# Reordering value products, transposes and a third gate-score broadcast in a windowed-attention and mixture-of-depths kernel

## The chip, the core and the metric

The kernel runs on one core of a Trainium2 chip. A core has five engines with separate instruction streams: TensorE (PE; its weight loads are shown as PEld), VectorE (DVE), ScalarE (ACT), GpSimd (POOL) and SyncE (SP, here only a DMA queue). TensorE writes to PSUM, a memory of 8 banks, from which VectorE or ScalarE fetch the results. The metric is the device time of one execution in microseconds. The profile is of a separate execution and is somewhat longer.

## What is computed

Two stages follow each other. The first is attention with a sliding window of 128 keys and 4 always visible "sink" keys, over 4 batches, 8 heads, 768 positions and 64 values per head:

```python
keep = (pos[None, :] < n_sink) | ((rel >= 0) & (rel < window))   # rel = query - key
scores = np.where(keep, scale * q @ k.T, -1e9)
a = softmax(scores)
x = a @ v                              # then heads side by side: [4, 768, 512]
```

The second stage picks, in each batch, the 128 positions with the highest gate score and adds a gated feed-forward result to those alone:

```python
scores = np.einsum('bsd,d->bs', x, w_gate)
top_idx = np.argpartition(-scores[b], 128)[:128]
ye = np.maximum(x[b, top_idx] @ w1, 0.0) @ w2          # 512 -> 1024 -> 512
out[b, top_idx] = x[b, top_idx] + sigmoid(scores[b, top_idx])[:, None] * ye
```

## The kernel before

The order of the work is written out by hand (`tc.manual_schedule`): each engine executes its instructions in the order in which the program calls them, and waits are set where data or buffers demand it.

**Steps.** The main loop (L619) has 30 steps. A step deals with one block j of 128 queries of one batch. Batch 0 is done in two passes over half of the heads (steps 0 to 5 and 6 to 11), batches 1 to 3 in one pass each (steps 12 to 17, 18 to 23, 24 to 29). In a step come, in this order on TensorE: the scores for the step two later (`step_scores`), the value products of the step (`values`), and then what is registered for the step in `todo` by `at(i, f)`, in the order of registration. Work is also hung in with `before` (ahead of the scores), `middle` (between scores and values) and `late` (at the step's end). VectorE normalises the values (`norm`, L290) straight after the value products, and the next step's value products need the same PSUM bank pair X, so they wait for this norm.

**Value products.** `values` (L253) multiplies in float32, which gives two matmul records for each call. First come the sinks (L272, tiles of 64x64), then products of full blocks (128 rows, 64 columns), and last the half blocks (64x64), which cover the edges of the window; half-block products also read the value chunk of block j+1.

**Transposes.** Keys and queries of two heads are cast to bf16 by `cast_pair` (L134), transposed on TensorE by `transposes` (L166) through banks Y and Y+1 and copied to `KT` and `QT` by VectorE (L177) or ScalarE (L179). The first scores of a batch, two steps ahead of its first block, need all of its pairs; the last pair is transposed at steps 9, 15 and 21. Ahead of the loop, pairs 0 and 2 of batch 0 are transposed with `fill` matmuls on zeros between, which keep TensorE busy.

**Ranking.** A position is chosen if fewer than 128 gate scores of its batch are higher. There are two ways to compare all 768 scores with all. For batches 0 and 1 the scores go out to a row in DRAM (`bounce_out`, L305) and come back broadcast over all partitions into `sbc` (`bounce_in`, L308), both through GpSimd's DMA queue; six `rank_c` (L311) on VectorE then count. For batches 2 and 3, `spread` (L315) broadcasts 128 scores by a TensorE matmul and a ScalarE copy to `sbl`, `compare` counts on VectorE, and `overtake` and `overtaken` add what later blocks contribute. `select` builds a one-hot matrix from the ranks, `choose` turns it into row numbers and starts the gather of the rows, and `ffn` hangs the feed-forward stages into three following steps. GpSimd's queue also loads the feed-forward weights (`load_weights`, before step 22), gathers and scatters.

Of the kernel before, what the change touches and what calls it, by code (L numbers as in the profile page):

```python
# [9 lines left out]
BF16 = mybir.dt.bfloat16  # L10
# [7 lines left out]
S = 768  # L18
D = 64
HP = H // 2  # L20
NB = S // 128
# [7 lines left out]
LO, HI, FULL = slice(0, 64), slice(64, 128), slice(0, 128)  # L29
# [4 lines left out]
def kernel(  # L34
# [14 lines left out]
    pe, dve, act, pool, sp = nc.tensor, nc.vector, nc.scalar, nc.gpsimd, nc.sync  # L49
# [6 lines left out]
    def one(shape, dt, name):  # L56
        return cp.tile(shape, dt, name=name, tag=name)
# [3 lines left out]
    X, Y = 4, 6  # L61
# [4 lines left out]
    raw = [one([128, 2, NB, D], FP32, f"raw{i}") for i in range(8)]  # L66
# [7 lines left out]
    xb = x0[:, 0:NB // 2, :].bitcast(BF16).rearrange("p a (t n) -> p (a t) n", t=2)  # L74
    E2 = x0[:, NB - 1, :].bitcast(BF16)[:, 0:NB * 128].rearrange("p (c n) -> p c n", n=128)
    sbc = one([128, S], FP32, "sbc")
    sbl = one([128, S], FP32, "sbl")
    G = one([128, 21 * 128], BF16, "G")
    junk = one([128, DM], FP32, "junk")
    less = one([128, NB], FP32, "less")  # L80
    rankl = [one([128, NB], FP32, "rankl"), x0[:, NB - 2, 40:40 + NB]]
    ones_b = one([128, 1], BF16, "ones_b")
    rank = one([128, NB], FP32, "rank")
    E = one([128, NB, 128], BF16, "E")
# [23 lines left out]
    srow = tc.dram_tile([B, S], FP32, name="srow")  # L108
# [12 lines left out]
    st = [State(b) for b in range(B)]  # L121
# [41 lines left out]
            sp.dma_start(out=vb[r, h0:h0 + 2, c, 0:D],  # L163
                         in_=v[0, 4 + h0:6 + h0, k0:k0 + 64, :].rearrange("h p d -> p h d"))

    def transposes(b, hp, bank):  # L166
        s = st[b]
        n = slot[(b, hp)]
        for t, (src, dst) in enumerate(((kq[2 * n], s.KT), (kq[2 * n + 1], s.QT))):
            trp = ps[:, bank + t, :].bitcast(BF16).rearrange("p (c n) -> p c n", c=8)  # L170
            for c in range(NB):
                pe.transpose(out=trp[:, c, :], in_=src[:, c, :, :].rearrange("p h d -> p (h d)"),  # L172
                             identity=ident_b[:, :])
            o = dst[:, hp, :].rearrange("d (p c) -> d p c", c=NB)
            i = trp[:, 0:NB, :].rearrange("d c p -> d p c")
            if t == 0 and (b == 0 or hp % 2 == 0):
                dve.tensor_copy(out=o, in_=i)  # L177
            else:
                act.copy(out=o, in_=i)  # L179

    def sink_keys(b, hp):
        s = st[b]
# [70 lines left out]
    def values(b, j, heads, bank, which):  # L253
        s = st[b]
        p = {i: ptn.get((b, i)) for i in (j - 1, j, j + 1)}
        seen = set()
        a, z = heads[0], heads[-1] + 1

        def mm(be, c, hh, rows, i, slot, kc):
            h = 4 * be + hh  # L260
            key = (be, c)
            pe.matmul(out=ps[64 * c:64 * c + 64, bank + be, hh * SK:hh * SK + SK],  # L262
                      lhsT=p[i][rows, h, 64 * slot:64 * slot + 64], rhs=s.v[be][rows, hh, kc, 0:SK],
                      start=key not in seen, stop=False, skip_group_check=True)
            seen.add(key)

        for be in range(2):
            for c in range(2):
                if j < 2 - c:
                    continue  # L270
                r = (LO, HI)[be ^ c]
                pe.matmul(out=ps[64 * c:64 * c + 64, bank + be, a * SK:z * SK],  # L272
                          lhsT=s.psk[which][r, c, 64 * (j - 1):64 * j], rhs=vsk[r, b, be, a:z, :],
                          start=True, stop=False, skip_group_check=True)
                seen.add((be, c))
        for hh in heads:
            if j:
                mm(0, 0, hh, FULL, j - 1, 2, j - 1)
            mm(0, 1, hh, FULL, j, 1, j)
        for hh in heads:  # L280
            mm(1, 0, hh, FULL, j, 1, j)
            mm(1, 1, hh, FULL, j, 2, j)
        for hh in heads:
            mm(0, 0, hh, LO, j, 0, j)
            mm(1, 1, hh, LO, *((j + 1, 0) if j < NB - 1 else (j, 3)), j + 1)
            if j:
                mm(0, 1, hh, HI, j - 1, 3, j - 1)
                mm(1, 0, hh, HI, j - 1, 3, j - 1)

    def norm(x, heads, bank):  # L290
        a, z = heads[0], heads[-1] + 1
# [14 lines left out]
        pool.dma_start(out=srow[b, :].rearrange("(p c) -> p c", c=NB), in_=st[b].scol[:, :])  # L306

    def bounce_in(b):  # L308
        pool.dma_start(out=sbc[:, :], in_=srow[b, :].partition_broadcast(128))

    def rank_c(b, c):  # L311
        dve.tensor_scalar(out=junk[:, :].bitcast(BF16)[:, 0:S], in0=sbc[:, :], scalar1=st[b].scol[:, c:c + 1],  # L312
                          scalar2=0.0, op0=ALU.is_gt, op1=ALU.add, accum_out=rank[:, c:c + 1])

    def spread(b, j, bank):  # L315
# [27 lines left out]
    def select(e, rk, c0, c1):  # L343
        n = c1 - c0
        dve.tensor_tensor(out=e[:, c0:c1, :], in0=iota_f[:, :].unsqueeze(1).to_broadcast((128, n, 128)),
                          in1=rk[:, c0:c1].unsqueeze(2).to_broadcast((128, n, 128)), op=ALU.is_equal)
# [23 lines left out]
    def gate_end(b):  # L370
        g = gt[b]
        dve.tensor_scalar_add(out=g[:, :], in0=g[:, :], scalar1=1.0)
        dve.reciprocal(out=g[:, :], in_=g[:, :])
# [38 lines left out]
    def scatter(b):  # L412
        pool.indirect_dma_start(out=flat[0:(b + 1) * S, :],
                                out_offset=bass.IndirectOffsetOnAxis(ap=idx[b][:, 0:1], axis=0),
                                in_=ys[b][:, :], in_offset=None, bounds_check=(b + 1) * S - 1, oob_is_err=False)

    with tc.manual_schedule():
# [24 lines left out]
        def fill(n):  # L442
            for i in range(n):
                pe.matmul(out=ps[:, i % 4, :], lhsT=zb[:, 0:128], rhs=zb[:, :], start=True, stop=True,
                          skip_group_check=True)
# [17 lines left out]
        cast_pair(0, 2, dve, act)  # L463

        fill(10)
        transposes(0, 0, Y)
        fill(5)
        transposes(0, 2, X)
        fill(2)

        steps = [(0, j, g) for g in range(2) for j in range(NB)]
        steps += [(b, j, None) for b in range(1, B) for j in range(NB)]
        todo = {}
# [3 lines left out]

        def at(i, f):
            todo.setdefault(i, []).append(f)

        def late(i, f):
            todo_late.setdefault(i, []).append(f)

        def middle(i, f):
            mid.setdefault(i, []).append(f)
# [47 lines left out]
        def choose(b, bank, e=E):  # L533
            keep[b] = chosen(b, bank, e)
            gate(b, keep[b])
            gather(b)

        def ranks(b, last):

            for j in range(last):  # L540
                at(start(b) + j + 1, lambda j=j: spread(b, j, 2))
                late(start(b) + j + 1, lambda j=j: compare(b, j))

        def overtaking(b, js, bank):
            overtake(js, bank)
            overtaken(b, js[-1], bank)


        for b, i, js in ((0, 12, (15, 15, 16, 17, 17, 18)), (1, 18, (20, 21, 22, 23, 24, 25))):
            middle(i, lambda b=b: bounce_out(b))  # L550
            middle(i + 1, lambda b=b: bounce_in(b))
            for c, i_c in enumerate(js):
                late(i_c, lambda b=b, c=c: rank_c(b, c))
        late(19, lambda: select(E, rank, 0, NB))
        at(20, lambda: choose(0, 3))
        at(21, lambda: gate_end(0))
        ranks(2, NB)
        at(25, lambda: overtaking(2, range(1, NB), 3))
        late(25, lambda: select(E, rank, 0, NB))
        at(26, lambda: choose(1, 3))  # L560
        late(26, lambda: select(E2, rankl[0], 0, NB))
        at(27, lambda: gate_end(1))
        at(27, lambda: choose(2, 3, E2))
        at(28, lambda: gate_end(2))
        for b in range(B - 1):
            at((12, 18, 24)[b], lambda b=b: token_cols(b))
        before(22, load_weights)
# [6 lines left out]
        for b, at_ in ((1, (0, 1, 2, 3)), (2, (6, 8, 9, 11)), (3, (13, 14, 15, 16))):  # L574
            for hp, i in enumerate(at_):
                before(i, lambda b=b, hp=hp: load_pair(b, hp))
        at(2, lambda: transposes(0, 1, Y))
        at(3, lambda: transposes(0, 3, Y))
        at(3, lambda: sink_keys(0, 1))
        at(3, lambda: sink_keys(0, 3))  # L580
        at(4, lambda: sink_scores(0, (1, 3), 1, Y))
        for b, i0 in ((1, 6), (2, 12), (3, 18)):
            for hp in range(HP):
                before(i0 + hp - 2, lambda b=b, hp=hp: cast_pair(b, hp))
                at(i0 + hp, lambda b=b, hp=hp: transposes(b, hp, Y))
                at(i0 + hp, lambda b=b, hp=hp: sink_keys(b, hp))
            at(i0 + 4, lambda b=b: sink_scores(b, range(HP), 0, Y))

        def ffn(b, i):
            before(i, lambda: ffn_cast(b))  # L590
            at(i, lambda: ffn_in(b, Y))
            at(i + 1, lambda: ffn_1(b, 0, Y + 1))
            at(i + 1, lambda: ffn_1(b, 1, Y))
            for half in range(2):
                at(i + 2, lambda half=half: ffn_2(b, half, Y + 1))
            at(i + 2, lambda: ffn_out(b, Y + 1))
        ffn(0, 24)
        ffn(1, 27)
        late(28, lambda: scatter(0))
        late(29, lambda: scatter(1))  # L600
        before(29, lambda: ffn_cast(2))
        at(29, lambda: ffn_in(2, Y))
# [12 lines left out]
                        in_=own4[0:16, :].unsqueeze(1).to_broadcast((16, 2 * B, HP)))  # L615
        pool.tensor_copy(out=vsk[64:80, :, :, :, :].rearrange("p b e h d -> p (b e h d)"),
                         in_=vsk[0:16, :, :, :, :].rearrange("p b e h d -> p (b e h d)"))
# [39 lines left out]
        b = B - 1  # L657
# [64 lines left out]
```

## Time and profile before

| | |
|---|---|
| time, median of 3 | 144.41 us (143.46 to 145.68) |
| span of the profiled execution | 149.5 us |
| TensorE granted clock, mean | 0.958 |
| DMA traffic | 32.42 MB, 217 GB/s on average |

How the stretches differ, in 10 us windows (engine busy us, and mean busy share of the 16 DMA engines):

| us | PE | DVE | ACT | DMA share |
|---|---|---|---|---|
| 0 to 10 | 5.84 | 6.43 | 3.65 | 0.87 |
| 30 to 40 | 8.40 | 6.43 | 6.57 | 0.99 |
| 60 to 70 | 8.18 | 6.14 | 5.99 | 0.95 |
| 80 to 90 | 9.62 | 9.18 | 7.00 | 0.69 |
| 100 to 110 | 7.62 | 8.69 | 5.13 | 1.02 |
| 120 to 130 | 9.79 | 7.35 | 3.28 | 0.49 |
| 140 to 150 | 3.46 | 1.36 | 1.20 | 0.24 |

Busy time of TensorE is modelled from pipelined matmuls, so gaps between the starts of its records tell more than its busy share. In a line of the timeline the columns are start and length in us, engine, line of the program, operation, tiles written and read, shapes, and how many records were merged; a bracket at the end tells how long the engine had been idle and who ended that. In a list of waits the three numbers are total us, how often, and the longest. Batch 0 ends near 48 us, batch 1 near 74, batch 2 near 101, the last value products near 129; the rest is the feed-forward work on the chosen rows of the last two batches.

### The profile page before, as it was taken

The numbers are of one execution on the slowest core, as the hardware profiler recorded it, in microseconds if no ns is written. First come the engines' busy times: TensorE is split into PE (matmuls) and PEld (weight loads), VectorE is DVE, ScalarE is ACT, GpSimd is POOL, SyncE is SP. The second block draws the span as 40 slices with busy tenths as digits, with TensorE's granted clock in tenths as the row PEclk, the third lists the DMA queues.
The fourth block names the chain that finished last, engine by engine and source line by source line (L and its number), as shares of the span: only waits on it lengthen the run. The fifth ranks groups of instructions, "written<-read, shape, count | busy, mean of one in ns | idle before, by whom it ended". The sixth has DMA issues, their size and how long they took to land. (4 is left out here: it accounts for less than half of the span.)

```text
span 149.5 us, 6406 instructions
## 1 busy us (share of the span) xinstructions
PE 122.4 (82%) x2759; PEld 93.0 (62%) x2759; DVE 90.3 (60%) x283; ACT 79.0 (53%) x106; POOL 60.8 (41%) x103
## 2 busy tenths in 40 slices
PE   6479798988779794968998997989599999987930
PEld 2146676677657682756776786768498578665700
DVE  6822145364835841637699898689882797576420
ACT  3064936666588756546665966566526243232310
POOL 8805902955275271109514633800130426550510
PEclk9956999999999999999999999999968999999997
DMA  3999959999999999997985664899950426441221
GB/s 97 373 195 360 237 144 365 393 222 273 280 292 364 359 285 349 351 292 218 256 229 149 178 196 150 115 181 230 273 189 12 153 95 203 189 175 39 52 91 70
DMA packets 41147, 32.42 MB, mean 217 GB/s; under 512 B 26768, under 2 KB 35984, under 8 KB 41120
## 3 DMA queue, kind: packets, MB, share of 16 engines
q1 hardware_dynamic: 37984, 26.22, 58.6%
q0 software_dynamic: 2592, 5.02, 14.9%
q10 hardware_dynamic: 544, 0.79, 1.5%
q8 instruction: 21, 0.34, 0.9%
q14 instruction: 6, 0.05, 0.1%
HBM read 25.20 MB, written 8.92 MB: 228 GB/s over the span
## 5 line engine op out<-in xcount | busy, mean ns | idle before, releaser
L262 PE MATMUL ps<-vbuf,pt 64*64 64x65 f32 (+1 forms) x1440 | 47.4, 227 | 7.6 <-issue 6.9
L262 PEld LDWEIGHTS ps<-vbuf,pt 64*64 64x64 f32 (+1 forms) x1440 | 40.1, 135 | 19.5 <-issue 15.5
L251 ACT ACTIVATE pt<-ps 128x1024 f32<-128x1024 f32 x48 | 47.3, 1033 | 6.9 <-PE ps L229 5.6
L295 DVE RECIPROCAL rz<-ps 128x8 f32<-128x8 f32 (+1 forms) x30 | 5.9, 198 | 39.0 <-PE ps L262 39.0
L186 POOL COPY ksk<-KT 64x4 bf16<-64x4 bf16 x32 | 9.3, 292 | 38.2 <-DVE KT L177 27.5
L141 POOL CAST kq<-raw 128x768 bf16<-128x768 f32 x28 | 22.6, 849 | 2.0 <-DMA raw<-in_k_dram 1.5
L213 PE MATMUL ps<-QT,KT 64*64 64x192 bf16 (+2 forms) x384 | 17.8, 249 | 5.1 <-ACT QT L179 2.4
L298 DVE TENSOR_TENSOR x<-ps,rz 128x256 f32<-128x256 f32 (+1 forms) x60 | 19.5, 366 | 1.2
L179 ACT COPY QT<-ps 128x768 bf16<-128x768 bf16 x16 | 12.8, 803 | 11.6 <-PE ps L172 11.6
L302 DVE CUSTOM_DVE_ANT_0 junk<-x,wgb 128x512 f32<-128x512 f32 x24 | 18.0, 751 | 0.4
L272 PE MATMUL ps<-vsk,psk 64*64 64x260 f32 (+1 forms) x180 | 15.6, 346 | 1.7 <-DVE x L298 1.4
L213 PEld LDWEIGHTS <-KT 64*64 64x64 bf16 x384 | 10.6, 108 | 10.3 <-issue 6.1
L172 PE MATMUL ps<-ident_b,kq 128*128 128x128 bf16 x192 | 14.6, 228 | 2.9 <-ACT kq L139 2.0
L229 PE MATMUL ps<-mask,ident_b 64*64 64x256 bf16 (+1 forms) x208 | 15.4, 263 | 0.0
L172 PEld LDWEIGHTS <-kq 128*128 128x128 bf16 x192 | 11.9, 102 | 4.9 <-ACT kq L139 2.2
L312 DVE TENSOR_SCALAR_CACHE_REDUCE junk<-sbc,scol 128x768 bf16<-128x768 f32 x12 | 12.2, 1013 | 0.4
L177 DVE COPY KT<-ps 128x768 bf16<-128x768 bf16 x10 | 9.5, 952 | 3.6 <-PE ps L172 3.6
L643 POOL CAST x<-x 128x512 bf16<-128x512 f32 x6 | 4.7, 790 | 15.8 <-DVE x L298 9.8
L395 PE MATMUL ps<-xeT,w_sb 128*128 128x128 bf16 x128 | 9.4, 239 | 0.7 <-ACT xeT L388 0.7
L318 ACT COPY sbl<-ps 128x128 f32<-128x128 f32 x12 | 3.1, 262 | 12.1 <-PE ps L316 12.1
L395 PEld LDWEIGHTS <-w_sb 128*128 128x128 bf16 x128 | 8.8, 109 | 1.1 <-DVE y L409 0.8
L272 PEld LDWEIGHTS ps<-vsk,psk 64*64 64x64 f32 x180 | 7.3, 132 | 3.1 <-DVE x L298 1.4
(93 smaller groups left out, 135.4 us busy)
## 6 DMA issues: line engine op xcount, KB each, us to landing
out_dram<-x SPq DMA_DIRECT2D x24, 256.0 KB, 4.8
raw<-in_k_dram SPq DMA_DIRECT2D x15, 384.0 KB, 4.7
raw<-in_q_dram SPq DMA_DIRECT2D x15, 384.0 KB, 6.6
vbuf<-in_v_dram SPq DMA_DIRECT2D x33, 128.0 KB, 5.0
w_sb<-in_moe_w_dram POOLq DMA_DIRECT2D x4, 512.0 KB, 9.6
xrow<-x SPq DMA_DIRECT2D x6, 256.0 KB, 2.3
vbuf<-in_v_dram SPq DMA_DIRECT2D x2, 384.0 KB
sbc<-srow POOLq DMA_DIRECT2D x2, 384.0 KB, 6.4
```

The lines of the kernel that those rows point to most:

```text
L141: (eng or pool).tensor_copy(out=o, in_=i)
L172: pe.transpose(out=trp[:, c, :], in_=src[:, c, :, :].rearrange("p h d -> p (h d)"), identity=ident_b[:, :])
L179: act.copy(out=o, in_=i)
L213: pe.matmul(out=sc[64 * m:64 * m + 64, e, a, o:o + n], lhsT=s.KT[r, hp, k0:k0 + 64], rhs=s.QT[r, hp, k0:k0 + n], start=a == 0, stop=False, ...
L229: pe.matmul(out=o, lhsT=ident_b[r, r], rhs=w[r].unsqueeze(1).to_broadcast((64, a.stop - a.start, 2, 64)), start=False, stop=True, skip_gro ...
L251: act.activation(out=po[:, gi, :, :, :], in_=sc[:, :, :, :], func=ACT.Exp, scale=0.125)
L262: pe.matmul(out=ps[64 * c:64 * c + 64, bank + be, hh * SK:hh * SK + SK], lhsT=p[i][rows, h, 64 * slot:64 * slot + 64], rhs=s.v[be][rows, h ...
L272: pe.matmul(out=ps[64 * c:64 * c + 64, bank + be, a * SK:z * SK], lhsT=s.psk[which][r, c, 64 * (j - 1):64 * j], rhs=vsk[r, b, be, a:z, :], ...
L298: dve.tensor_tensor(out=xo[:, e, :, :], in0=xg[:, e, :, 0:D], in1=rz[:, e, 0:n, :].to_broadcast((128, n, D)), op=ALU.mult)
L302: dve.tensor_tensor_reduce(out=junk[:, :], in0=x, in1=wgb[:, :], scale=1.0, scalar=0.0, op0=ALU.mult, op1=ALU.add, accum_out=st[b].scol[:, ...
L312: dve.tensor_scalar(out=junk[:, :].bitcast(BF16)[:, 0:S], in0=sbc[:, :], scalar1=st[b].scol[:, c:c + 1], scalar2=0.0, op0=ALU.is_gt, op1=A ...
L395: pe.matmul(out=hps[:, f, :], lhsT=w1_sb[:, dc, fc * 128:(fc + 1) * 128], rhs=xeT[:, dc, :], start=(dc == 0), stop=(dc == 3), skip_group_c ...
```

## The change

It has four edits. (1) In `values`, the half-block products move from the end to straight behind the sinks, so that all work in 64x64 tiles stands together. (2) `transposes` is put at the head of a step's `todo` list (`first`), straight behind the values; for batches 1 to 3 the pairs whose keys VectorE copies are the odd ones instead of the even ones, so that at the last pair the two copies are on two engines. (3) Ahead of the loop, four fill matmuls move between the key and the query transposes of the first pair, in place of five behind them. (4) The third batch (b = 2) is ranked through DRAM, as batches 0 and 1: its scores leave in the middle of step 24, the broadcast is issued at the end of that step into the freed buffer `raw[0]`, the six counts stand in steps 25 to 27; the spreads, comparisons and overtaking of that batch go. The second batch's selection, its feed-forward stages and the first scatter come one step earlier, the third batch's choice and gather one step later.

```diff
+    sbcs = [sbc, sbc, raw[0][:, :, :, :].rearrange("p h c d -> p (h c d)")]
...
-    def transposes(b, hp, bank):
+    def transposes(b, hp, bank, between=None):
...
-            if t == 0 and (b == 0 or hp % 2 == 0):
+            if t == 0 and (b == 0 or hp % 2):
                 dve.tensor_copy(out=o, in_=i)
             else:
                 act.copy(out=o, in_=i)
+            if between and t == 0:
+                between()
...
         for hh in heads:
+            mm(0, 0, hh, LO, j, 0, j)
+            mm(1, 1, hh, LO, *((j + 1, 0) if j < NB - 1 else (j, 3)), j + 1)
+            if j:
+                mm(0, 1, hh, HI, j - 1, 3, j - 1)
+                mm(1, 0, hh, HI, j - 1, 3, j - 1)
+        for hh in heads:
             if j:
                 mm(0, 0, hh, FULL, j - 1, 2, j - 1)
             mm(0, 1, hh, FULL, j, 1, j)
         for hh in heads:
             mm(1, 0, hh, FULL, j, 1, j)
             mm(1, 1, hh, FULL, j, 2, j)
-        for hh in heads:
-            mm(0, 0, hh, LO, j, 0, j)
-            mm(1, 1, hh, LO, *((j + 1, 0) if j < NB - 1 else (j, 3)), j + 1)
-            if j:
-                mm(0, 1, hh, HI, j - 1, 3, j - 1)
-                mm(1, 0, hh, HI, j - 1, 3, j - 1)
...
-        transposes(0, 0, Y)
-        fill(5)
+        transposes(0, 0, Y, lambda: fill(4))
         transposes(0, 2, X)
...
-        for b, i, js in ((0, 12, (15, 15, 16, 17, 17, 18)), (1, 18, (20, 21, 22, 23, 24, 25))):
+        for b, i, js in ((0, 12, (15, 15, 16, 17, 17, 18)), (1, 18, (20, 21, 22, 23, 24, 24)),
+                         (2, 24, (25, 25, 26, 26, 27, 27))):
             middle(i, lambda b=b: bounce_out(b))
-            middle(i + 1, lambda b=b: bounce_in(b))
+            (late if b == 2 else middle)(i + (b < 2), lambda b=b: bounce_in(b))
...
-        ranks(2, NB)
-        at(25, lambda: overtaking(2, range(1, NB), 3))
-        late(25, lambda: select(E, rank, 0, NB))
-        at(26, lambda: choose(1, 3))
-        late(26, lambda: select(E2, rankl[0], 0, NB))
-        at(27, lambda: gate_end(1))
-        at(27, lambda: choose(2, 3, E2))
-        at(28, lambda: gate_end(2))
+        late(24, lambda: select(E, rank, 0, NB))
+        at(25, lambda: choose(1, 3))
+        at(26, lambda: gate_end(1))
+        late(27, lambda: select(E2, rank, 0, NB))
+        at(28, lambda: choose(2, 3, E2))
+        at(29, lambda: gate_end(2))
...
-                at(i0 + hp, lambda b=b, hp=hp: transposes(b, hp, Y))
+                first(i0 + hp, lambda b=b, hp=hp: transposes(b, hp, Y))
...
-        ffn(1, 27)
-        late(28, lambda: scatter(0))
+        ffn(1, 26)
+        late(27, lambda: scatter(0))
```

## The prediction

> **What bounds the kernel now.** I read the page's first two parts, then the waits, then the windows, and last the timeline around single steps. A step is one pass of the main loop (steps 0 to 29).
>
> The page and the list of waits (columns: total us, times, longest):
>
> ```profile
> PE 122.4 (82%) x2759; PEld 93.0 (62%) x2759; DVE 90.3 (60%) x283; ACT 79.0 (53%) x106; POOL 60.8 (41%) x103
> ...
> q8 instruction: 21, 0.34, 0.9%
> ...
> DVE rz L295 <- PE ps L262: 39.0, 26, 4.3
> PEld ps L262 <- issue: 15.5, 32, 2.3
> ACT sbl L318 <- PE ps L316: 12.1, 8, 3.0
> PE ps L213 <- ACT QT L179: 2.4, 3, 0.8
> ```
>
> TensorE sets the pace: VectorE waits 39.0 us for value products, while TensorE rarely waits for a named engine. Most of its idle time is "issue". Part of that is the change of tiling; the larger holes (1.2 us before 64.50, 1.75 before 108.18) end 2.3 to 2.6 us after a 16 KB packet starts on q8, the queue of instructions. The change does not remove them, it shuffles where they fall.
>
> The timeline of TensorE around one step, matmuls and then weight loads; forms of one line are merged, so the 64 are 32 full and 32 half-block records:
>
> ```profile
> 68.03 0.68 PE L272 MATMUL ps<-vsk,psk 64*64 64x260 f32 x8
> 68.64 1.78 PE L262 MATMUL ps<-vbuf,pt 128*64 128x65 f32 x64
> 70.34 0.46 PE L196 MATMUL ps<-QT,ksk 128*64 128x320 bf16 x4
> ...
> 68.63 1.64 PEld L262 LDWEIGHTS ps<-vbuf,pt 128*64 128x64 f32 x64 [0.39 <-issue]
> ```
>
> The single records: last sink to first full product 0.309 us, 32 full ones over 0.931, then 0.152 to the halves, 32 halves over 0.478 (four at a time, 58 ns apart), then 0.150 to the next 128x128 work. Halves followed by scores, both 64x64, are 0.006 apart.
>
> The start, on ScalarE, and the late part on GpSimd and VectorE:
>
> ```profile
> 7.42 1.56 ACT L139 CAST kq<-raw 128x768 bf16<-128x768 f32 x2 [4.28 <-DMA raw<-in_q_dram]
> 12.58 0.80 ACT L179 COPY QT<-ps 128x768 bf16<-128x768 bf16 x1 [2.61 <-PE ps L172]
> ...
> 92.86 1.52 POOL L526 DMA_DIRECT2D w_sb<-in_moe_w_dram  x2
> 94.37 1.53 POOL L530 DMA_DIRECT2D w_sb<-in_moe_w_dram  x2
> ...
> DMA to landing us min/median/max: 11.0/12.9/14.8
> ...
> 111.73 0.96 DVE L345 TENSOR_TENSOR E<-iota_f,rank 128x768 bf16<-128x768 f32 x1
> 115.91 0.21 DVE L295 RECIPROCAL rz<-ps 128x8 f32<-128x8 f32 x1 [2.76 <-PE ps L262]
> ```
>
> The landing line is that of the two w2 loads (L530): the last lands 14.8 us after its issue at 95.12, so GpSimd's DMA queue is full from 92.9 to 109.9.
>
> [...]
>
> **The change part by part**, on the profile's clock (span 149.5).
>
> *Start.* Q's first transposes wait for ScalarE's cast until 8.30; five fills then run at the half clock (0.43 each), and pair 2's transposes begin at 11.05. Now four fills run in the hole before 8.30, and pair 2 follows at once. ScalarE's casts end at 8.98, then two QT copies of 0.80: 10.6 instead of 13.38. First scores 13.32 to about 10.7: 2.6 us. The values' loads bound this; the last of the first group lands at 11.45, about when they would be wanted.
>
> *Halves behind the sinks.* Full step: 0.309 + 0.931 + 0.152 + 0.478 = 1.87 becomes about 0.108 (one sink pass, 260 columns in the same mode) + 0.478 + 0.152 + 0.931 = 1.67, so 0.20 less; half-width step (batch 0) by the same rows 0.15 less. If scores follow, full-to-scores costs a drain of 0.15 that half-to-scores did not, so only steps with 128-row work behind the values keep all, or those where the next sinks wait for the norm. To step 21: 8 half-width steps 1.2, nine full 1.8, five bound by the norm 0.7. Sum 3.7. The halves read the value chunk of block j+1 one microsecond earlier; it lands steps ahead (5 us after an issue four steps earlier).
>
> *Transposes first, and odd pairs' K on VectorE.* At the three batch turns the scores wait for two 0.80 copies in a row on ScalarE (gaps of 0.70, 1.05 and 1.06). Side by side, K's copy of 0.95 starts on VectorE only after the norm (1.0), so I take 0.3 each, 0.6 before the weights are issued. Queued behind it are the gate score and then the next norm, two microseconds away: hidden. At step 20 a wait of 0.40 for VectorE falls away.
>
> *Third batch through DRAM.* Removed: six spreads at 0.325 of TensorE, six ScalarE copies of 0.26 (hidden), 15 overtaking products (0.39), six comparisons on VectorE (0.34 to 1.01, with their small ones 5.5). Added: six ranks at 1.01 + 0.08 = 6.6 on VectorE, packed into steps 25 to 27, and two DMAs. Three spreads lie before the weights: 1.0.
>
> *The added wait.* The scores leave at step 24 and come back from GpSimd, behind the weights in the same queue. Count from the first weight issue, W (92.86 now). The weights drain at W+17. The small transfer lands at about W+17.2, the broadcast is issued at W+17.4 and needs 3.6 to 4.8 (the two of before: 55.41 to 61.78 on busy engines, 83.0 to about 87.7): W+21 to W+22.2. VectorE reaches the first rank (end of step 25) at about W+15.7: two steps of 3.2, one of 3.7 by norm and ranks, one of 6 with the first FFN product. It then stands about 6 us. Behind it: the other rank, a comparison, and step 26's norm, for which step 27's sinks wait. GpSimd too stands between, with the second batch's gather behind it, and TensorE waits for that at its FFN transposes until W+22.7. So step 26's norm ends at W+21.6+2.2+0.5+1.0 = W+25.3; now it ends at 116.91, W+24.04. Loss 1.3 against before. Step 27 then holds gate end 0.3, output 0.75, gate score 0.77, two ranks 2.2, comparison 0.62 ahead of its norm, 5.6 against 5.2 now: 0.4 more. In the tail the third gather comes later, but the second FFN's last product (1.75) has left it: I set 0.4 more. Together +2.1.
>
> *Sum.* To W: 2.6 + 3.7 + 0.6 + 0.4 + 1.0, less 0.4 since the key copies that GpSimd makes before the weights now wait for VectorE: 7.9. Holes in the instruction stream and norms take some; I keep four fifths, 6.3. Then 149.5 - 6.3 + 2.1 = 145.3. The timed median is 144.41 for a profile of 149.5, a factor of 0.966: 140.4.
>
> **The rivals.** *The broadcast arrives in time* (it slips between the weights, or they drain faster in unprofiled runs): VectorE does not stand, step 26's norm ends near W+19.4, 5.9 earlier than above: 139.4, or 134.7 timed. For it: no run shows a small transfer queued behind the weights. [...] *The wait and the crowding of VectorE eat all* (steps 25 to 27 become VectorE's, TensorE falls to the lower clock after standing, as it did from 109.76 for 3.4 us): gain 4, loss 4, 144.4, not slower, no gain. For it: VectorE is busy 6.76 of the 8.00 us from 101.5 to 109.5 already. *Slower*: early gains vanish in data waits (DMA share is 0.95 to 1.08 from 20 to 70) and fetch holes, and the wait stays: gain 1, loss 5, 153.5, or 148.3. Against: no transposes of batches 1 to 3 wait for a cast, so data is ahead.
>
> **How the numbers follow.** Forecast 0.5, early broadcast 0.12, no gain 0.27, slower 0.11. An early gain of 4 to 8 and a loss of 0.7 to 4 give 136.7 to 144.4 alone; with part of the outer cases, 135.5 to 145.2. The forecast lies near the 2% line (141.5), so some of it falls within 2%, and part of the no-gain case falls below it: faster 0.6, same 0.28, slower 0.12.
>
> **What would show it.** First scores near 10.7; a value block of about 1.67 with one drain; TensorE gaps at the batch turns down by 0.3; the weights issued near 86.5; a VectorE wait of 4 to 7 us at the first rank of the third batch, released by the broadcast, and a GpSimd wait for the small transfer. No such wait, or scores starting after 12, would make the prediction wrong.

## The result, and the profile after

The changed kernel takes 152.36 us (151.06 to 154.34, 4 runs) beside 145.05 us (143.46 to 146.38, 4 runs) for the kernel before on the same chip: a ratio of 1.055, 95% interval 1.038 to 1.073. It is slower; 140.4 was predicted, and the range ended at 145.2. Medians and ranges, here and below, are of all runs, while ratios compare only the fast runs, those within 1.5% of the fastest of their kernel.

The profile of before that the prediction worked from (span 149.5 us) is of an execution of 151.22 us, over 4% longer than its timed median, while the profile after (span 149.2 us) is of an execution of 151.06 us, the fastest of its four. The two spans, 0.3 us apart, therefore hide a difference of 7 us, and another profile of the kernel before is shown beside them (run e1 below, span 146.6, of an execution of 148.33 us, still 1.7 above e1's median).

From the page of the kernel after (engine busy time; two groups: busy us, mean ns of one, then the engine's idle time before them and who ended most of it):

```profile
PE 119.5 (80%) x2731; PEld 96.4 (65%) x2731; DVE 90.6 (61%) x276; ACT 77.4 (52%) x100; POOL 62.8 (42%) x105
...
L142 POOL CAST kq<-raw 128x768 bf16<-128x768 f32 x28 | 23.7, 854 | 15.3 <-DMA raw<-in_k_dram 11.8
...
L315 DVE TENSOR_SCALAR_CACHE_REDUCE junk<-raw,scol 128x768 bf16<-128x768 f32 x6 | 6.1, 1013 | 7.6 <-DMA raw<-srow 7.4
```

From the waits of the kernel after (total us, times, longest):

```profile
POOL raw L312 <- DMA srow<-scol: 8.9, 1, 8.9
DVE junk L315 <- DMA raw<-srow: 7.4, 1, 7.4
```

TensorE is 2.9 us less busy than in the profile of before, but only 1.4 less than in e1 (120.9), and run e2 below has 116.2 with more work on it; so this busy time tells little. The two waits are new: GpSimd stands 8.9 us for the third batch's small transfer, VectorE 7.4 us for its broadcast. The cast line holds a surprise: GpSimd now waits 15.3 us for raw keys and queries to land, where the profile of before had 2.0.

The start in the kernel after (timeline; ScalarE, then TensorE's first scores):

```profile
7.11 1.57 ACT L140 CAST kq<-raw 128x768 bf16<-128x768 f32 x2 [3.97 <-DMA raw<-in_q_dram]
8.58 1.49 ACT L180 COPY QT<-ps 128x768 bf16<-128x768 bf16 x2
...
9.60 0.28 PE L216 MATMUL ps<-QT,KT 64*64 64x192 bf16 x4
```

The two QT copies follow the casts at once, and the first scores start at 9.60 instead of 13.32 (e1 has 12.08, and run e3, whose start is that of before, 10.50). Now the late part, in order of time; the landing line belongs to the two w2 loads (L535):

```profile
89.51 1.52 POOL L531 DMA_DIRECT2D w_sb<-in_moe_w_dram  x2
91.01 1.53 POOL L535 DMA_DIRECT2D w_sb<-in_moe_w_dram  x2
...
96.48 0.57 POOL L309 DMA_DIRECT2D srow<-scol  x1 [3.14 <-DVE scol L305]
...
107.16 0.61 PE L275 MATMUL ps<-vsk,psk 64*64 64x260 f32 x8
107.60 1.72 PE L265 MATMUL ps<-vbuf,pt 64*64 64x65 f32 x64
107.89 0.56 POOL L312 DMA_DIRECT2D raw<-srow  x1 [8.93 <-DMA srow<-scol]
108.83 1.06 POOL L380 DMA_INDIRECT xe<-out_dram,idx  x1 [0.37 <-issue]
109.25 0.49 PE L319 MATMUL ps<-ident_f,scol 128*128 128x128 f32 x2
...
112.04 1.01 DVE L315 TENSOR_SCALAR_CACHE_REDUCE junk<-raw,scol 128x768 bf16<-128x768 f32 x1 [7.43 <-DMA raw<-srow]
112.67 0.61 POOL L385 CAST xeb<-xe 128x512 bf16<-128x512 f32 x1 [2.16 <-DMA xe<-out_dram,idx]
...
113.34 0.40 PE L390 MATMUL ps<-ident_b,xeb 128*128 128x128 bf16 x4 [1.88 <-POOL xeb L385]
...
114.49 0.20 DVE L298 RECIPROCAL rz<-ps 128x8 f32<-128x8 f32 x1
...
DMA to landing us min/median/max: 12.6/14.1/15.5
```

The last weight load was issued at about 91.8 and landed 15.5 us later, at about 107.25. The small transfer, issued at 96.48, landed 11.1 us later, at 107.6; those of the first two batches needed 5.1 and 5.4. The broadcast was issued at 107.89 and VectorE's first rank began at 112.04. Step 26's value products were finished at about 109.3 (107.60 + 1.72), but their norm started at 114.49, since it stands behind the ranks in VectorE's program: the products waited 5.2 us.

Where each step stands, by the start of its norm (us from the start of the span):

| | before | e1 (before, again) | after |
|---|---|---|---|
| step 0 | 16.80 | 15.69 | 13.69 |
| step 12 | 49.99 | 46.37 | 45.13 |
| step 18 | 78.34 | 74.51 | 73.75 |
| first weight issue, W | 92.86 | 91.87 | 89.51 |
| step 25 | 108.91 | 107.60 | 102.62 |
| step 26 | 115.91 | 113.01 | 114.49 |
| step 28 | 124.93 | 122.04 | 125.14 |
| end of the span | 149.51 | 146.62 | 149.19 |

A lead of 5.0 us on e1 at step 25 turns into a lag of 1.5 at step 26 and 3.1 at step 28. Against e1 the change is behind; against the longer profile of before it seems level. The lead at step 25 is partly chance: run e8 below, the kernel before with some more instructions at the start, is there at 103.05.

### The profile page after: what moved, and what is told of

Its sections match the earlier page's. It is cut to its first block, busy times and chain, and to the rows that moved or that the text cites. A ratio compares the mean times of both kernels' runs of the same rounds, so it can differ in the third digit from the quotient of the medians.

```text
span 149.2 us, 6325 instructions
## 1 busy us (share of the span) xinstructions
PE 119.5 (80%) x2731; PEld 96.4 (65%) x2731; DVE 90.6 (61%) x276; ACT 77.4 (52%) x100; POOL 62.8 (42%) x105
## 5 line engine op out<-in xcount | busy, mean ns | idle before, releaser
L265 PE MATMUL ps<-vbuf,pt 128*64 128x65 f32 (+1 forms) x1440 | 51.2, 226 | 9.7 <-issue 8.9
L265 PEld LDWEIGHTS ps<-vbuf,pt 128*64 128x64 f32 (+1 forms) x1440 | 46.5, 137 | 15.0 <-issue 9.8
L142 POOL CAST kq<-raw 128x768 bf16<-128x768 f32 x28 | 23.7, 854 | 15.3 <-DMA raw<-in_k_dram 11.8
L275 PE MATMUL ps<-vsk,psk 64*64 64x260 f32 (+1 forms) x180 | 16.1, 346 | 2.3 <-DVE x L301 1.7
L305 DVE CUSTOM_DVE_ANT_0 junk<-x,wgb 128x512 f32<-128x512 f32 x24 | 17.2, 717 | 0.4
L216 PEld LDWEIGHTS <-KT 64*64 64x64 bf16 x384 | 10.0, 108 | 7.6 <-issue 3.0
L398 PE MATMUL ps<-xeT,w_sb 128*128 128x128 bf16 x128 | 10.1, 250 | 0.7 <-ACT xeT L391 0.7
L315 DVE TENSOR_SCALAR_CACHE_REDUCE junk<-raw,scol 128x768 bf16<-128x768 f32 x6 | 6.1, 1013 | 7.6 <-DMA raw<-srow 7.4
L398 PEld LDWEIGHTS <-w_sb 128*128 128x128 bf16 x128 | 9.5, 114 | 1.2 <-issue 0.8
L232 PEld LDWEIGHTS <-ident_b 64*64 64x64 bf16 x208 | 7.8, 111 | 0.9 <-issue 0.9
```

The costliest lines, as they stand in the source:

```text
L142: (eng or pool).tensor_copy(out=o, in_=i)
L216: pe.matmul(out=sc[64 * m:64 * m + 64, e, a, o:o + n], lhsT=s.KT[r, hp, k0:k0 + 64], rhs=s.QT[r, hp, k0:k0 + n], start=a == 0, stop=False, ...
L232: pe.matmul(out=o, lhsT=ident_b[r, r], rhs=w[r].unsqueeze(1).to_broadcast((64, a.stop - a.start, 2, 64)), start=False, stop=True, skip_gro ...
L305: dve.tensor_tensor_reduce(out=junk[:, :], in0=x, in1=wgb[:, :], scale=1.0, scalar=0.0, op0=ALU.mult, op1=ALU.add, accum_out=st[b].scol[:, ...
L398: pe.matmul(out=hps[:, f, :], lhsT=w1_sb[:, dc, fc * 128:(fc + 1) * 128], rhs=xeT[:, dc, :], start=(dc == 0), stop=(dc == 3), skip_group_c ...
```

## The experiments

### Which edit makes it slower

e1 is the kernel before, run as a kernel of its own. e2 is the changed kernel with the third batch ranked as before, e3 the kernel before with that edit alone, e4 the changed kernel with the two transfers of that batch on SyncE's queue.

```diff
# e2, against after (e3 is the reverse, against before)
-                         (2, 24, (25, 25, 26, 26, 27, 27))):
+        ranks(2, NB)
+        at(25, lambda: overtaking(2, range(1, NB), 3))
...
# e4, against after
-        pool.dma_start(out=srow[b, :] ...
+        (sp if b == 2 else pool).dma_start(out=srow[b, :] ...
-        pool.dma_start(out=sbcs[b][:, :] ...
+        (sp if b == 2 else pool).dma_start(out=sbcs[b][:, :] ...
```

> The kernel before, unchanged, for a profile whose time agrees with its timed runs: the profile on hand had a span of 149.5 us where the runs take 145.05, and the changed kernel's profile, 149.2, is one of its own timed runs (151.06). Both theories: a time of 144 to 146, a span near 143.5. Queue theory (the slowdown is the third batch's broadcast queued behind the weight loads): the steps before the weights are 2 to 4 us earlier than in the profile on hand, and step 25 to step 26 takes about 6 to 7 us between norms, against 11.87 in the changed kernel. Early-loss theory (the first three edits gain nothing or lose in ordinary runs): its norms of steps 10 to 25 are as early as those of the changed kernel, or earlier.

> The changed kernel with the third batch ranked on TensorE and the late schedule as before: only the half blocks' place, the transposes' place and the start are changed. Queue theory: the wait is gone, so it is faster than the kernel before, by 2 to 6 us (139 to 143). Early-loss theory: 145 to 150, no better than before.

> The kernel before with only the third batch's path through DRAM and the late schedule that goes with it. Queue theory: 148 to 153, with a VectorE wait of 5 to 8 us at the first rank of the third batch, ended by the broadcast. Early-loss theory: 144 to 148, since the six spreads saved pay for a part of the wait.

> The changed kernel with the third batch's two transfers issued by SyncE's queue instead of GpSimd's; all else as in the change. Queue theory: the small transfer no longer stands behind the weights, both land within 8 to 10 us of step 24's start, VectorE waits under 3 us, and the time falls by 4 to 7 us to 145 to 148. If instead the DMA engines as such are too busy, or the crowding of VectorE in steps 25 to 27 is the cost, the time stays at 150 or more.

Measured, the kernel before at 146.05 on that chip: e1 146.66 (ratio 0.995, 0.989 to 1.001), e2 146.62 (144.26 to 147.58), e3 153.48 (ratio 1.050, 1.040 to 1.060), e4 149.54 (145.5 to 151.86). The third batch's edit alone costs as much as the whole change; the other three edits together neither cost nor bring anything that these runs show. The waits of e3 from 90 to 135 us are of the same kind as those of the kernel after:

```profile
POOL raw L310 <- DMA srow<-scol: 7.3, 1, 7.3
...
DVE junk L313 <- DMA raw<-srow: 6.5, 1, 6.5
```

From step 25's norm to the end of the span, e1 takes 39.0 us and e2 38.7, e3 46.5 and the kernel after 46.6: the edit costs 7.5 to 7.9 us there. Of it 5.5 and 6.6 lie between the norms of steps 25 and 26 (10.89 against 5.41 without the other edits, 11.87 against 5.25 with them), the wait itself; 1.7 and 1.4 between those of 27 and 28 (5.47 against 3.79 and 4.05), where two ranks and the one-hot comparison of `select` now stand before the norm on VectorE. Up to step 25 it brings 3.1 to 4.8 us (102.62 against 105.75, 102.79 against 107.60), more than the 1.0 of three spreads; part of that is chance, as e2 and e1 had stretches just there in which TensorE stood ("holes", below).

In e4 step 25 to 26 takes 5.26 us again, which speaks for the queue. But TensorE stood for 3.62 us from 94.3 in its profile, which put step 25 at 106.55, 3.9 us later than in the kernel after, and gave the transfer that much more time. So e4 alone doesn't settle it; e5 and e10 below do.

### Loading the weights earlier

If the small transfer waits behind the weights, loading them two steps earlier should free the queue in time. e5 does that in the changed kernel (the first edit below lets them start after an earlier load of the last batch's values).

```diff
-                    after(i, arrived[(B - 1, 5)])
+                    after(i, arrived[(B - 1, 4)])
...
-        before(22, load_weights)
+        before(20, load_weights)
```

> The changed kernel with the feed-forward weights loaded two steps earlier, before step 20 instead of step 22, so that GpSimd's queue is free when the third batch's scores leave; nothing else moved. Queue theory: small transfer and broadcast land within about 10 us of step 24's start, VectorE's wait at the first rank of the third batch falls from 7.4 us to under 2, and the time falls by 4 to 7 us, to 145 to 148. Crowding theory (steps 25 to 27 are too full on VectorE anyway): the wait goes, but the time stays at 149 or more.

It took 161.95 us (159.52 to 163.53) beside 144.75, a ratio of 1.132 (1.086 to 1.178). GpSimd's timeline and two of the waits in e5:

```profile
87.57 1.50 POOL L535 DMA_DIRECT2D w_sb<-in_moe_w_dram  x2
89.37 1.11 POOL L380 DMA_INDIRECT xe<-out_dram,idx  x1 [0.30 <-issue]
...
104.07 0.65 POOL L189 COPY ksk<-KT 64x4 bf16<-64x4 bf16 x3 [13.36 <-DMA xe<-out_dram,idx]
...
PE ps L199 <- POOL ksk L189: 13.7, 1, 13.7
POOL ksk L189 <- DMA xe<-out_dram,idx: 13.4, 1, 13.4
```

The wait at the third batch's transfer is gone, but the weights now stand in front of the first batch's gather: issued at 89.37, it lets the sink keys go on only at 104.07, and TensorE waits 13.7 us for those. The third batch's row, now alone in the queue, landed 1.8 us after its issue at 111.10. So two different transfers issued behind the weights came late in this queue: the row of the kernel after (11.1 us from issue to landing) and the gather of e5 (14.6 us).

### Do the blocks of instructions decide

A hole is a stretch in which TensorE stands and the profile names nothing that it waits for. Most of the larger holes end shortly after a 16 KB packet ("block of instructions" here) starts on the queue of instructions, which has 21 packets, 0.34 MB, on the pages of before and after: of 104 holes over 0.6 us in the 18 profiles (between the starts of successive matmul records, from 12 us on), 97 end 2.1 to 3.3 us after one, nearly all of them 2.2 to 2.7 (by chance about a sixth would). Many packets are followed by none. Such a hole in e1 (TensorE's timeline; the value products of step 15, cut in two by 2.1 us):

```profile
57.23 0.80 PE L262 MATMUL ps<-vbuf,pt 128*64 128x65 f32 x18
60.13 1.30 PE L262 MATMUL ps<-vbuf,pt 128*64 128x65 f32 x46 [2.11 <-issue]
```

e6 is the kernel before with the half-block products moved, e7 to e10 are e2, before, after and e4 with 118 more TensorE instructions at the start (the padding). By the author's estimate they move every boundary between blocks by about half a block: 2,759 matmuls and as many weight loads beside 21 packets are some 260 to a packet. No view shows the boundaries themselves.

```diff
# e7 to e10
-        fill(10)
+        fill(5)
+        for i in range(64):
+            pe.matmul(out=ps[0:64, i % 4, 0:64], lhsT=zb[LO, 0:64], rhs=zb[LO, 0:64], ...
```

> The kernel before with the half-block products behind the sinks alone. Drain theory: each step of batches 1 to 3 that is not held by anything else is 0.1 to 0.2 us shorter between norms, 3 to 4 us in all, and the time falls to 142 to 143. Fetch theory (what the order saves, TensorE spends standing for its instructions): the steps without a hole are shorter by the same amount, but the sum of holes that end 2.2 to 2.7 us after an instruction packet grows from 9 to 11 us to 12 or more, and the time stays at 145 to 147.

> [...] Fetch theory: where the block ends fall decides the holes, so their sum and the time differ from those of the kernel without the padding (14.2 us of holes, 146.6) by 2 us or more, either way. If holes depend on the amount of work alone, they stay at 13 to 15 us and the time within 1 us.

> The kernel before with the same padding of 118 instructions. Fetch theory: the sum of holes moves away from 9 to 11 us, more likely up, and the time with it, by 1 us or more. If holes depend on the amount of work alone: 9 to 11 us of holes, and a time within 1 us of the kernel before.

> The whole change, with the padding of 118 instructions at the start that took the first three edits from 146.6 to 142.5 us. Queue theory: the padding moves the holes of the instruction stream as it did there, by 2 to 5 us, but the wait of 7 us at the third batch's broadcast stays: 148 to 151, still slower than the kernel before. If holes were the main cause of the slowdown: 145 or less.

> The whole change, the third batch's transfers on SyncE's queue, and the padding. Queue theory: neither the wait nor the worst holes: 143 to 147. What is left over the first three edits with the padding (142.5) is the crowding of VectorE in steps 26 to 28, which took 1.2 + 1.7 us more than in the kernel before, less the spreads saved. If crowding cost nothing, 141 to 142.

Measured, with the sum of the holes over 0.35 us that end 2.0 to 3.3 us after a packet's start (e1: 8.9 us, e2: 14.2, e3: 9.0, after: 12.6; other bounds move a sum by up to 3 us):

| | median us (range) | before, same chip | ratio (95%) | holes, us |
|---|---|---|---|---|
| e6 | 145.62 (141.32 to 147.43) | 144.75 | none | 7.5 |
| e7 | 142.48 (140.93 to 144.58) | 144.75 | 1.001 (0.991 to 1.011) | 7.6 |
| e8 | 144.76 (139.34 to 147.0) | 144.75 | none | 5.8 |
| e9 | 151.05 (150.57 to 152.1) | 146.56 | 1.045 (1.036 to 1.053) | 8.1 |
| e10 | 146.89 (143.48 to 150.65) | 146.56 | 0.993 (0.980 to 1.007) | 7.2 |

Three things follow. The changed kernel stays slower with the padding (e9, ratio 1.045), so, if the estimate holds, the place of the boundaries isn't what makes it slow. With SyncE's queue (e10) it is level with before: by the medians of e9 and e10 the other queue is worth 4 us, by their ratios 5%. Yet e10 isn't free of the transfer; from its timeline (SyncE's queue, then VectorE):

```profile
94.88 0.33 SPq L309 DMA_DIRECT2D srow<-scol  x1
101.65 0.33 SPq L312 DMA_DIRECT2D raw<-srow  x1
...
106.30 1.01 DVE L315 TENSOR_SCALAR_CACHE_REDUCE junk<-raw,scol 128x768 bf16<-128x768 f32 x1 [3.03 <-DMA raw<-srow]
```

The broadcast follows the small transfer by 6.8 us even there, VectorE waits 3.0, and the crowding of VectorE stays: 6.29 us from step 26 to 27 (5.24 before), 5.47 from 27 to 28. And the move of the half blocks alone (e6) shortens the steps that wait for nothing else, but not the time.

e8 and e9 also show where the loss lies, since both have the 118 instructions more and their profiles are of executions (144.47 and 150.57 us) near their medians. Up to step 25's norm e9 leads by 3.0 us (100.04 against 103.05), and from there to the end it takes 48.7 against 39.7. Of these 9.0 us, 5.6 lie between the norms of steps 25 and 26, 1.0 between those of 27 and 28, and 2.9 behind the norm of step 29 (21.9 against 19.0). Three lines of e9 and e8: a wait of e9, then the transposes of the third batch's gathered rows on TensorE in each:

```profile
DVE junk L315 <- DMA raw<-srow: 7.7, 1, 7.7
...
129.13 0.61 PE L390 MATMUL ps<-ident_b,xeb 128*128 128x128 bf16 x4 [1.94 <-POOL xeb L385]
...
125.70 0.39 PE L387 MATMUL ps<-ident_b,xeb 128*128 128x128 bf16 x4
```

The third batch's choice and gather come one step later in the change, and TensorE stands 1.94 to 1.96 us for the gathered rows in all six kernels with that edit (after, e3, e4, e5, e9, e10) and in none of the others. In all of the six but e5 its granted clock then falls to half, within 2 us, for 3.4 to 6.8 us (0.50 from 133.3 to 136.7 us in the kernel after); that the standing is the cause isn't shown. From the norm of step 29 to the end these five take 20.0 to 21.9 us and the twelve others 18.9 to 20.0.

### Transposes first

e11 is e2 with the transposes and the parity of the pairs as before, so that only the half blocks and the start are changed; e12 is the same with the 118 instructions.

```diff
-            if t == 0 and (b == 0 or hp % 2):
+            if t == 0 and (b == 0 or hp % 2 == 0):
...
-                first(i0 + hp, lambda b=b, hp=hp: transposes(b, hp, Y))
+                at(i0 + hp, lambda b=b, hp=hp: transposes(b, hp, Y))
```

> Half blocks behind the sinks and the moved fills, but the transposes where they were and the even pairs' keys on VectorE as before; third batch on TensorE. With the transposes first, TensorE waited for the ScalarE copy of the spread scores before the next scores (1.4 us in three waits from 74 to 100), since that copy stood behind the copies of the transposes and the spread uses the scores' bank. If that is what the first three edits lose late, this is 1 to 2 us faster than they are together: 144 to 145.5. Fetch theory: the holes decide, 142 to 147, and no third batch wait of either kind.

> The same with the padding. Drain theory: with holes of 6 to 10 us the earlier start (2 us) and the saved drains (3 us) show in full: 139.5 to 142, faster than the kernel before by over 2%. Fetch theory: it may as well fall on a bad place, 143 to 146.

e11 took 146.25 us (142.34 to 147.84) and e12 145.09 (ratio 0.999, 0.989 to 1.009), the kernel before 146.56. The ratios of e12 and e7 (1.001) lie within each other's intervals: putting the transposes first brings nothing measurable. One price shows in the waits of e2 between 74 and 100 us:

```profile
PE ps L216 <- ACT sbl L321: 1.4, 3, 0.7
```

The scores now follow so close behind the spread, whose bank they use, that TensorE waits for ScalarE's copy of it. e11 and e12 have no such wait and are no faster than e2 and e7, so it does not show in the time.

### Why the shorter steps bring no time

All profiles show the earlier start and the shorter steps, and all are level again by step 18: its norm starts between 72.4 and 74.5 us in every kernel but the first profile of before, though step 0's started anywhere from 13.5 to 16.5. From 20 to 70 us the DMA engines are nearly full (mean busy share 0.85 to 1.03 in the 10 us windows of e1). The last four runs leave out the K and Q loads of batches 1 and 2 (the casts read what batch 0 left), 6.3 MB of 32.4: e13 in the kernel before, e14 in e2, e15 in e8, e16 in e7.

```diff
-        for b, at_ in ((1, (0, 1, 2, 3)), (2, (6, 8, 9, 11)), (3, (13, 14, 15, 16))):
+        for b, at_ in ((3, (13, 14, 15, 16)),):
```

> The kernel before, without the loads of K and Q of batches 1 and 2 (their casts read what batch 0 left in the raw buffers; 6.3 MB less to move). Theory A, the stretch from 20 to 70 us is paced by the DMA engines, which delay both raw rows and blocks of instructions: step 18 begins well before the 74.2 to 78.3 of the kernel before, near 69, the TensorE holes that end 2.2 to 2.7 us after a block of instructions shrink in that stretch, and the time falls by 4 us or more. Theory B, the DMA engines have no part in it, the stretch is paced by TensorE and by holes that fall at random: the same times within 1 us, step 18 near 74.

> The changed kernel without its third-batch edit, and without the loads of K and Q of batches 1 and 2. Theory A: with the DMA engines out of the way the start's lead of 2 us and the shorter steps are kept, step 18 begins 4 us or more ahead of the same cut in the kernel before, and the time is lower than that one by 3 to 5 us. Theory B: step 18 within 1 us of it, the times within 1 us.

> The same cut in the kernel before with the 118 more instructions of TensorE at the start, which shift where the blocks of instructions end. Theory A: within 1.5 us of the cut kernel without them, since a block that arrives in time leaves no hole wherever its boundary falls. Theory B: 2 us or more apart, as the two kernels were with their loads.

> The cut and the more instructions in the changed kernel without its third-batch edit. Theory A: within 1.5 us of the cut one without them, less 0 to 1.4 at the start that the more instructions cost, and 3 us or more below the cut kernel before with them. Theory B: no lead over that one beyond 1 us.

The kernel before took 144.68 us on that chip.

| | e13 (before) | e14 (e2) | e15 (before, more instructions) | e16 (e7) |
|---|---|---|---|---|
| median us | 139.4 | 137.66 | 138.44 | 136.99 |
| range | 138.82 to 144.2 | 134.38 to 138.81 | 138.17 to 140.47 | 135.37 to 138.3 |
| norm of step 0 | 13.77 | 13.25 | 13.79 | 13.26 |
| norm of step 18 | 69.38 | 65.53 | 69.36 | 66.97 |
| holes | 3.7 | 2.2 | 3.2 | 2.7 |

GpSimd's casts in e1, e2, e13 and e14, from the pages:

```profile
L141 POOL CAST kq<-raw 128x768 bf16<-128x768 f32 x28 | 23.6, 867 | 8.7 <-DMA raw<-in_k_dram 6.8
```
```profile
L142 POOL CAST kq<-raw 128x768 bf16<-128x768 f32 x28 | 24.4, 887 | 16.8 <-DMA raw<-in_k_dram 13.6
```
```profile
L141 POOL CAST kq<-raw 128x768 bf16<-128x768 f32 x28 | 23.1, 868 | 0.9 <-DMA raw<-in_k_dram 0.2
```
```profile
L142 POOL CAST kq<-raw 128x768 bf16<-128x768 f32 x28 | 24.1, 901 | 1.0 <-DMA raw<-in_q_dram 0.4
```

And three windows of e1, then of e13 (window, its length, busy us of PE, PEld, DVE, ACT, POOL, granted clock, DMA share, GB/s):

```profile
30.00:40.00 10.00, 9.23 (x246) 7.62 (x246) 7.65 (x31) 8.18 (x10) 5.28 (x12) 1.00 0.85 220
40.00:50.00 10.00, 9.38 (x261) 7.41 (x261) 5.44 (x18) 8.06 (x10) 4.14 (x6) 1.00 1.01 316
50.00:60.00 10.00, 6.97 (x202) 5.50 (x194) 4.10 (x11) 5.99 (x7) 4.89 (x11) 1.00 0.94 281
```
```profile
30.00:40.00 10.00, 9.23 (x260) 7.53 (x264) 6.72 (x31) 8.42 (x11) 6.90 (x14) 1.00 0.53 156
40.00:50.00 10.00, 9.55 (x272) 7.68 (x262) 6.38 (x20) 8.15 (x11) 6.47 (x11) 1.00 0.72 202
50.00:60.00 10.00, 8.90 (x262) 7.26 (x258) 6.13 (x15) 7.79 (x9) 3.84 (x9) 1.00 1.08 325
```

Theory A holds in its first half. With less to move, the kernel before alone gains 5 us (ratio 0.971, 0.958 to 0.983); TensorE's holes shrink from 5 to 14 us (all kernels with their loads) to 2 to 4; the casts hardly wait. So two things shrink with the traffic, the casts' waits for rows (8.7 to 0.9 us, e1 and e13) and the holes behind the packets (8.9 to 3.7 us); these runs lessen both at once and do not tell how much each is worth. Its second half holds in part. At step 18 the three edits now lead by 3.9 and 2.4 us, where they led by 0.4 (e2 on e1) and 1.7 (e7 on e8). That is less than the 4 us expected, at least in the second pair: the start's lead shrinks to 0.5 us at step 0 (from 2.2 and 1.0), since the kernel before starts earlier too, and the medians differ by 1.7 and 1.5 us only, not by 3 to 5; with ranges as wide as these, that much is not told from the 0.0 and 2.3 of the pairs with their loads. So it is shown that the level falls with the DMA traffic (step 18 at 74.51 in e1, 69.38 in e13), and not shown how much of the edits' lead they take.

## Why the prediction was wrong

In the prediction's own terms: of the 6.3 us to be gained ahead of the weights the runs show 0 (e2) to 2.3 (e7) in the time, and in place of the 2.1 us to be lost behind them the third batch's edit costs about 7 (e3). The mechanism of the loss was right; its size was taken against a profile that already held part of it.

**What was right.** The added wait came where it was placed, in the order described and at nearly the time given: the weights drained at W + 17.7 (predicted W + 17), the small transfer landed at W + 18.1 (W + 17.2), the first rank began at W + 22.5 (the broadcast at W + 21 to W + 22.2), step 26's norm ended at about W + 26.0 (W + 25.3). VectorE stood 7.4 us (6). The first scores start at 9.60, where 10.7 was given; but the 2.6 us that they were to gain was read from a profile whose TensorE ran at half its clock there (granted 0.50 from 7.4 to 14.1 us), and at the full clock the edit is worth about 1 us (10.50 in e3, 10.15 in e13; 9.60 after, 9.15 in e14). The steps' gain is as worked out: steps free of other waits shrink by 0.18 in batch 0 (2.27 to 2.09; predicted 0.15) and by 0.15 to 0.25 later (step 22 to 23, 3.90 in e8 to 3.67 in e7; predicted 0.20). The block of step 26 above, from its sinks at 107.16 to the next work in 128-row tiles at 109.25, takes 2.09 where the one shown of before took 2.31. One change between 64x64 tiles and tiles of 128 rows fewer fits most of this: such a change took 0.152 us from the full products to the halves in the trace of before, and 0.148 from the halves to the full products in the trace after. This gap is the "drain" of the recorded texts; what TensorE does in it isn't shown. Two terms that the sums use no run had shown. The 0.108 from the last sink to the first half block is 0.209 in the single records of step 26 after, against 0.309 from the last sink to the first full product before. And W + 17.2 takes it that a row behind the weights lands just after them; in the kernel after it did so, at 107.6, some 0.35 us after the last weight load.

**The factor 0.966 failed.** The prediction is 12.0 us short of the 152.36. On the profile's clock it gave 145.3 and the span after is 149.2, 3.9 off; the rest comes with the factor, which would have turned even the true 149.2 into 144.1, 8.2 short. It is no mechanism of its own: it hid that the profile is of an unusually long execution. It took 144.41 over 149.5 as a constant between profile and timed run, but both spans lie 1.7 to 1.9 us below the times of their own executions (151.22 and 151.06). The excess of the first profile was no scale: part of it was holes at places that the change touches, as the next point shows.

**"Loss 1.3 against before" failed by its baseline.** From W to the end the prediction gave 56.65 + 2.1 = 58.75, and the kernel after took 59.68: 0.9 off. What was wrong was the 56.65 as the measure of before: e1 takes 54.75, e2 53.86 and e8 52.94. The profile of before had a 1.75 us hole ahead of 108.18 and a lower granted clock from 109.76 (0.50 for 3.4 us), both noted in the prediction and both in the very stretch that the wait replaces, so about half of what the wait costs was already counted as old. From the norm of step 24 to that of step 26 it took 12.5 us, e1 9.8. So step 26's norm was to end 1.3 later than the W + 24.0 of before; in e1 and e8 it ends at W + 22.1 and W + 20.8, and the true delay is 3.9 to 5.2. Against e1 and e2 the loss from W on is 4.9 and 5.8 us, not 2.1; for e9 against e8 it is 8.4.

Two smaller terms of the same sum were mis-sized as well. The crowding of VectorE, 0.4, was put between the norms of steps 26 and 27, where nothing is lost (5.18 against 5.24); it comes between those of 27 and 28, which the sum left out, with 1.4 to 1.7 in e3 and after and 1.0 in e9. And the tail, set at 0.4 because the second FFN's last product had left it, holds the wait of 1.9 to 2.0 us for the third gather; it is longer by up to 2.9 us (e9 against e8).

**"I keep four fifths, 6.3" failed.** W came at 89.51, not at 86.5: 3.4 ahead of the profile of before, 2.4 of e1, and e8 has 89.82 without any of the edits, e3 88.11 without the first three. The pieces were there, but the stretch from 20 to 70 us isn't TensorE's alone. "No transposes of batches 1 to 3 wait for a cast, so data is ahead" was read from one profile, the longest of before, in which data had time to be ahead. In e1 GpSimd's casts already wait 8.7 us for rows, in e2 16.8. The wait moved to the loads, as far as these waits show, and the three edits together bring between nothing (e2) and 2.3 us (e7), within what separates runs.

**The rivals.** The one that ends slower named both causes (holes and data waits early, the wait late) with a gain of 1 and a loss of 5, and was given 0.11. On the timed runs the gain is about 0 and the loss about 7. (A slip beside it: a gain of 8 and a loss of 0.7 give 137.4, not 136.7, as the lower end.)

**Blocks of instructions.** The holes that end behind the start of a packet sum to 5 to 14 us in a run, and to 2 to 4 with 6.3 MB less to move. The prediction took them as shuffled by the change, and that they are (1.75 us between matmul starts ahead of 108.18 in before, 1.90 ahead of 85.97 in the kernel after): they do not decide (e9 is slower by 1.045, e8 and e9 having sums of 5.8 and 8.1 us).

## What to carry to other kernels

A small transfer has to be looked at with what stands ahead of it in its queue: here 3 KB behind 2 MB of weights took nearly 6 us longer (11.1 against 5.1 and 5.4), and moving the 2 MB ahead of a gather cost more (13.4 us of waiting in e5). Before a delay is priced against a profile, look whether the profile already holds an accidental hole there, and whether its execution took as long as the timed runs. TensorE time saved in a stretch with full DMA engines (here a mean busy share of 0.85 to 1.03, e1) is time to be proved, not counted.

## What the runs showed of the hardware

- Of 104 TensorE holes over 0.6 us in 18 profiles, 97 end 2.1 to 3.3 us after the start of a 16 KB packet of instructions. With a fifth less DMA traffic the sums of such holes over 0.35 us fall from between 5.2 (e12) and 14.2 us (e2) to between 2.2 and 3.7.
- On GpSimd's queue a 3 KB row issued behind the weight loads landed 11.1 us after its issue (after, where the last weight load landed at 107.25 and the row at 107.6; e3 too) and 12.0 (e9), against 3.4 to 6.2 for the rows of the first two batches and 1.8 with the queue empty (e5). A gather issued behind them took 14.6 us (e5), against 3.3 to 7.9 elsewhere, and GpSimd's next work waited 13.4.
- On SyncE's queue the same row needs 6.0 (e4) and 6.8 us (e10) to the issue that waits for it while the weights move, against 1.8 with GpSimd's queue empty (e5), so the second queue didn't make it free here.
- Ahead of the loop TensorE's granted clock falls to half in some profiles of the start of before and not in others: in before (0.50 from 7.4 to 14.1 us), e1, e6 and e8, but not in e3, with the same start and all loads, nor in e13 and e15, without the loads of batches 1 and 2. So the DMA load alone doesn't decide it. None of the eleven kernels with the changed start shows it; what decides, these runs don't tell. The granted clock in tenths, 40 slices of the span, in e1 and e3:

```profile
PEclk9959999999999999999999997899999999999996
```
```profile
PEclk9999999999999999999999999999999999978995
```
